# A gated linear recurrence feeding an exact-GELU feed-forward layer: decay totals by DMA, two units loaded by chunks, one PSUM pool, a new order

## The chip, the cores and the metric

The kernel runs on one core of one Trainium2 chip. The metric is the time of one execution on the device in microseconds (us), inputs and output in the chip's memory. Five engines work side by side, each on its own list of instructions in order: TensorE (PE, matmuls), VectorE (DVE), ScalarE (ACT), GpSimd (POOL) and SyncE (SP). In this kernel SP does nothing but issue DMAs, and an SP instruction that waits holds back every DMA listed behind it.

## The reference

```python
def _attn_ref(q, k, v, f_logit):              # (4, 8, 768, 48) each
    B, H, S, D = q.shape
    f = 1.0 / (1.0 + np.exp(-f_logit))
    state = np.zeros((B, H, D, D), dtype=np.float32)
    y = np.zeros_like(q)
    for t in range(S):
        state = f[:, :, t, :, None] * state + np.einsum('bhd,bhe->bhde', k[:, :, t], v[:, :, t])
        y[:, :, t] = np.einsum('bhd,bhde->bhe', q[:, :, t], state)
    return y

def _moe_ref(x, w_in, w_out):                 # (3072, 384), (384, 2048), (2048, 384)
    h = x @ w_in
    g = 0.5 * h * (1.0 + erf(h / np.sqrt(2.0)))
    return g @ w_out

x = attn_out.transpose(0, 2, 1, 3).reshape(B * S, H * D)   # then _moe_ref(x, ...)
```

## The kernel before

**Tiling.** The 4 x 768 tokens make 24 chunks of 128 tokens, six to a batch, numbered 0 to 23; two chunks make a unit, 0 to 11, so each batch has three units and the state starts anew with units 0, 3, 6 and 9. Unit u is also group u of the feed-forward part.

**One unit's attention.** `decays(u)` takes exp and ln of the logits (E, L; lines 559 and 561), and PE sums the logarithms along the chunk with a triangular matrix (C; line 585, or 590 and 591). ACT makes two factors from the sums, `rg` = exp(-G) (RG, line 607) and `gt` = exp(G) (GT, line 613). k times rg and q times gt go to `sc` (KP and QP, line 640, on DVE, a few on POOL), v becomes bf16 `vb` (VC, line 647, mostly POOL). `turn` brings `sc` into `kq` with channels on the partitions: for units 0 to 3 by PE transposes (line 876) and a copy from PSUM, for units 4 to 11 by a transposing DMA from SP (KD, line 864). From `kq` PE makes the scores (A), DVE masks them (AM, line 901), and PE multiplies them with `vb` (Y). The state goes on: PE forms k'v (S), DVE adds the old state (R, line 925), POOL multiplies by the decay total of the chunk, `gl` (T, line 927), and POOL copies the result as bf16 `sb` (SB, line 932), which the next chunk's Y takes up (line 969 on PE). The first chunk of a batch has no old state, and DVE multiplies by `gl` at once (R, line 921). `yb` is the bf16 copy of Y (YB, line 945); it is turned into `xT` by PE and a copy (XT and X, lines 961 and 964) or by a transposing DMA (XD, line 949, units 5 to 11).

**Decay totals.** For a chunk that stands with its tokens on the partitions, four matmuls with one column each (line 587) put the totals, channel by channel, into the PSUM bank of C, and ACT takes their exp into `gl` (line 629). Units in `PAIRS` (0 to 4) are loaded differently: partition p holds tokens 2p and 2p+1 of the unit, which makes one transfer of 384 KB per input with runs of 384 bytes (line 513). Their sums, scores and products have forms of their own: 590 and 591, totals at 579 with ACT at 634, scores at 1058 or 1061, S at 1093 (1085 in batch 0), Y at 1113, the old state at 975 or 978. The other units take two transfers of 192 KB per input, with runs of 192 bytes (line 521).

**Feed-forward.** Group g's 256 tokens go through two rounds: F1 (line 1165) in 8 tiles of 6 matmuls with 256 columns, each followed by one GELU on ACT (GE, line 1175), and F2 (line 1186) in 4 parts of 4 matmuls for each chunk, then a copy (O, line 1191) and a store (line 1200). After a unit in `PAIRS` the GELU also puts the tokens back in order. ACT's exp/ln and GELU lie in two tables, and each change of table is an instruction (line 1248).

**What sets the order.** Every piece of work is recorded with `P.add` (engine, planned duration, reads, writes, buffers), and `Plan.run` places the pieces one after another in the order of the numbers in `ORDER`. The instructions of each engine then stand in that order, and the plan's times also choose which buffer a piece gets. The planned durations and landing times (`d`, `lat`, `lag`) act on nothing else. PSUM has eight banks, `BANKS = (4, 0, 4)`: four for the feed-forward part and some early tiles (`s_fh`), four for all else (`s_m`, also used as `s_ap`). Loads are issued on SP in the order of `LOADS`; the weights come by POOL's DMAs (win at 525, wout at 528), and the first load of unit 3 waits until the third piece of wout, o3, has landed. At the start, while PE waits for data, line 1241 fills it with matmuls on a `junk` tile.

Of the kernel before, what the change touches and what calls it, by code (L numbers as in the profile page):

```python
# [11 lines left out]
ALU = mybir.AluOpType  # L12
# [9 lines left out]
TURN = 0.1  # L22
# [5 lines left out]
BANKS = (4, 0, 4)  # L28
# [47 lines left out]
class Plan:  # L76
# [30 lines left out]
    def run(self):  # L107
# [16 lines left out]
        while ready:  # L124
# [63 lines left out]
PAIRS = [0, 1, 2, 3, 4]  # L188
# [30 lines left out]
SBT = []  # L219
AHEAD = 4.4  # L220
UNITS = 12
WARM = 30.0
# [39 lines left out]
def kernel(  # L262
# [56 lines left out]
    s_gt, s_rg = slots(3, [C, HD], F32, "gt"), slots(3, [C, HD], F32, "rg")  # L319
# [13 lines left out]
    s_fh, s_m = Slots(nf, banks[:nf]), Slots(8 - nf - na, banks[nf + na:])  # L333
# [34 lines left out]
    P.add("POOL", 1.9, pair_sums, wr=["trip", "negp"], prio=-100)  # L368
    P.add("POOL", 2.6, pair_mask, wr=["maskp"], prio=-85)
# [9 lines left out]
    for i in range(6):  # L379
        P.add("DVE", 0.07, lambda i=i: nc.vector.memset(s_gl.tiles[i], 1.0), wr=[f"glz{i}"], prio=-60)  # L380
    z_gl = [f"glz{i}" for i in range(6)]
    z_lf = [f"lfz{i}" for i in range(3)]
# [24 lines left out]
    def load(eng, issue, wr, bufs, dur, name):  # L407
# [22 lines left out]
        if prev is not None and eng != "act" and order[-1][0] != eng:  # L430
            prev.lat = 2.2
# [18 lines left out]
        if 7 <= i and o.lat < 1.8:  # L450
            o.lat = 2.0 if name == "i0" else 1.8 if i < 30 else 1.7
# [23 lines left out]
    for what in LOADS:  # L475
# [12 lines left out]
        elif what[0] in "ucfkqv":  # L488
# [13 lines left out]
            elif x["pair"]:  # L502
                assert what[0] != "c"
                for nm, a in names:
                    if what[0] not in ("u", nm[0]):
                        continue
                    if nm == "fl" and m in SPLIT:
# [7 lines left out]
                        [(nm, 2 * m), (nm, 2 * m + 1)], [x[nm]], 1.5, f"{nm}{m}")  # L515
            else:
                for j in js:
                    for nm, a in names:
                        if what[0] not in ("u", "c", nm[0]):
                            continue  # L520
                        load("sp", lambda x=x, nm=nm, a=a, m=m, j=j: nc.sync.dma_start(
                            out=half(m, x[nm], j), in_=src(a, 2 * m + j)),
                            [(nm, 2 * m + j)], [x[nm]], 1.05, f"{nm}{m}.{j}")
        elif what[0] == "i" and m < len(WIN):
            load("pool", lambda m=m: nc.gpsimd.dma_start(out=win[m], in_=win_src[:, :, wcol[m]:wcol[m] + WIN[m]]),
                 [f"win{m}"], [], {512: 2.4, 1024: 4.1}[WIN[m]] + (0.3 if order[-1][0] == "sp" else 0.0), what)
        elif what[0] == "o":
            load("pool", lambda m=m: nc.gpsimd.dma_start(out=wout[m], in_=wo_src[m]), [f"wout{m}"], [], 2.15, what)


    def decays(u):
# [32 lines left out]
        g1d, gld = pair and u in G1D, u in GLD  # L564
# [717 lines left out]
```

## Time and profile before

| | |
|---|---|
| time of three runs | 179.1, 179.34, 180.19 us (median 179.34) |
| profiled execution | span 178.1 us; of its time no more is recorded than this span |
| PE, ACT, DVE, POOL busy | 168.7, 130.0, 93.7, 55.2 us |
| PE instructions | 1996 matmuls, 1996 weight loads |
| F1 and F2 (lines 1165, 1186) | 576 and 368 matmuls, 69.0 and 67.0 us busy |
| GELU | 96, 57.2 us busy |
| table changes on ACT | 17, and one load at the start, 1.283 us each |
| DMA | 32.61 MB in 106997 packets, 102112 of them under 512 bytes |

The page gives the busy time of each engine, the chain of work that ended last, and groups of instructions by line of the code. Matmuls overlap, so the busy time of a group of matmuls is more than what the group adds to PE's list; the pieces of the chain, which run from start to start, tell that. "idle before, releaser" says what an engine waited for.

### The profile page before, as it was taken

The numbers are of one execution on the slowest core, as the hardware profiler recorded it, in microseconds if no ns is written. First come the engines' busy times: TensorE is split into PE (matmuls) and PEld (weight loads), VectorE is DVE, ScalarE is ACT, GpSimd is POOL, SyncE is SP. The second block draws the span as 40 slices with busy tenths as digits, with TensorE's granted clock in tenths as the row PEclk, the third lists the DMA queues.
The fourth block names the chain that finished last, engine by engine and source line by source line (L and its number), as shares of the span: only waits on it lengthen the run. The fifth ranks groups of instructions, "written<-read, shape, count | busy, mean of one in ns | idle before, by whom it ended". The sixth has DMA issues, their size and how long they took to land.

```text
span 178.1 us, 4916 instructions
## 1 busy us (share of the span) xinstructions
PE 168.7 (95%) x1996; PEld 131.2 (74%) x1996; DVE 93.7 (53%) x188; ACT 130.0 (73%) x221; POOL 55.2 (31%) x119
## 2 busy tenths in 40 slices
PE   7787889999997999999999999999999999999993
PEld 2345679866787787886688689866797976887972
DVE  5188750067988556338677681246582276560110
ACT  2954399967797999989477597786684789951630
POOL 7267595041126801501052334002222504410000
PEclk9999999999999999999999999999999999999999
DMA  5999999999979898988999999999899975405412
GB/s 140 261 261 214 277 179 195 213 221 256 235 154 227 187 212 188 202 178 169 233 174 248 188 174 204 188 220 156 191 238 179 232 165 81 85 4 112 138 60 88
DMA packets 106997, 32.61 MB, mean 183 GB/s; under 512 B 102112, under 2 KB 106080, under 8 KB 106976
## 3 DMA queue, kind: packets, MB, share of 16 engines
q1 hardware_dynamic: 105056, 29.07, 79.0%
q0 software_dynamic: 1776, 3.15, 10.0%
q8 instruction: 15, 0.25, 0.6%
q10 hardware_dynamic: 144, 0.10, 0.2%
q14 instruction: 6, 0.05, 0.1%
HBM read 25.17 MB, written 4.72 MB: 168 GB/s over the span
## 4 chain that ended last, share of the span: by engine, by line
PE 72%; DMA 14%; SPq 6%; POOL 3%; issue 1%; DVE 1%; ACT 0%; DVEq 0%; POOLq 0%
PE ps L1165 30%; PE ps L1186 29%; DMA vt<-in_v_dram 6%; SPq L513 4%; DMA kt<-in_k_dram 4%; DMA kq<-sc 3%; PE ps L995 2%; PE ps L1031 2%; PE ps L1211 1%; DMA out_dram<-osb 1%; PE ps L585 1%; PE ps L969 1%; SPq L949 1%; SPq L1200 1%; POOL vb L647 1%
## 5 line engine op out<-in xcount | busy, mean ns | idle before, releaser
L1175 ACT ACTIVATE gT<-ps 128x512 bf16<-128x512 f32 x96 | 57.2, 665 | 18.4 <-PE ps L1165 17.6
L1165 PE MATMUL ps<-xT,win 128*128 128x256 bf16 x576 | 69.0, 273 | 0.8 <-DMA win<-in_moe_w_in_dram 0.7
L1186 PE MATMUL ps<-wout,gT 128*128 128x384 bf16 x368 | 67.0, 326 | 0.0
L1165 PEld LDWEIGHTS <-win 128*128 128x128 bf16 x576 | 61.7, 114 | 3.7 <-DMA win<-in_moe_w_in_dram 0.9
L1186 PEld LDWEIGHTS <-gT 128*128 128x128 bf16 x368 | 34.1, 98 | 18.7
L901 DVE TENSOR_TENSOR am<-ps,mask 128x512 bf16<-128x512 f32 x28 | 17.5, 683 | 18.5 <-PE ps L995 18.5
L1248 ACT ACT_TABLE_LOAD x17 | 21.8, 1283 | 0.3
L640 DVE TENSOR_TENSOR sc<-kt,rg 128x384 bf16<-128x384 f32 x19 | 11.5, 606 | 15.8 <-ACT rg L607 11.1
L1191 DVE COPY osb<-ps 128x384 f32<-128x384 f32 x20 | 10.7, 552 | 16.8 <-PE ps L1186 15.7
L927 POOL TENSOR_TENSOR tn<-rr,gl 128x384 f32<-128x384 f32 x12 | 10.7, 889 | 25.1 <-DVE rr L925 19.1
L647 POOL CAST vb<-vt 128x384 bf16<-128x384 f32 x18 | 9.5, 539 | 26.8 <-DMA vt<-in_v_dram 26.6
L901 DVE TENSOR_TENSOR am<-ps,maskp 128x512 bf16<-128x512 f32 x20 | 12.7, 683 | 5.3 <-PE ps L1061 3.8
L945 DVE CAST yb<-ps 128x384 bf16<-128x384 f32 x21 | 11.4, 555 | 7.6 <-PE ps L1031 5.6
L640 DVE TENSOR_TENSOR sc<-qt,gt 128x384 bf16<-128x384 f32 x20 | 13.3, 684 | 3.4 <-ACT gt L613 2.7
L558 ACT ACTIVATE fl<-fl 128x768 f32<-128x768 f32 x12 | 10.1, 842 | 5.0 <-DMA fl<-in_f_logit_dram 5.0
L932 POOL CAST sb<-tn 48x192 bf16<-48x192 f32 x30 | 10.7, 362 | 8.3 <-DVE tn L921 7.1
L613 ACT ACTIVATE gt<-ps 128x384 f32<-128x384 f32 x21 | 10.3, 495 | 3.8 <-PE ps L587 2.9
L607 ACT ACTIVATE rg<-ps 128x384 f32<-128x384 f32 x21 | 10.1, 494 | 3.5 <-PE ps L587 2.9
L640 POOL TENSOR_TENSOR sc<-kt,rg 128x384 bf16<-128x384 f32 x5 | 5.3, 1065 | 22.5 <-ACT rg L607 14.3
L561 ACT ACTIVATE lf<-fl 128x768 bf16<-128x768 f32 x12 | 10.2, 849 | 0.3
L925 DVE TENSOR_TENSOR rr<-ps,tn 128x384 f32<-128x384 f32 x12 | 6.7, 555 | 5.9 <-PE ps L1018 4.8
L1241 PE MATMUL ps<-junk 128*128 128x512 bf16 (+3 forms) x26 | 8.3, 448 | 1.3 <-POOL junk L1233 1.3
(85 smaller groups left out, 145.1 us busy)
## 6 DMA issues: line engine op xcount, KB each, us to landing
out_dram<-osb SPq DMA_DIRECT2D x19, 192.0 KB, 2.8
kt<-in_k_dram SPq DMA_DIRECT2D x14, 192.0 KB, 4.5
fl<-in_f_logit_dram SPq DMA_DIRECT2D x14, 192.0 KB, 3.9
vt<-in_v_dram SPq DMA_DIRECT2D x14, 192.0 KB, 3.9
qt<-in_q_dram SPq DMA_DIRECT2D x14, 192.0 KB, 3.7
fl<-in_f_logit_dram SPq DMA_DIRECT2D x5, 384.0 KB, 4.9
kt<-in_k_dram SPq DMA_DIRECT2D x5, 384.0 KB, 6.2
qt<-in_q_dram SPq DMA_DIRECT2D x5, 384.0 KB, 6.3
```

The lines of the kernel that those rows point to most:

```text
L613: P.add("ACT", 0.40, lambda g=gps[j], gtv=gtv: nc.scalar.activation(gtv(), g.t()[:, 0:HD].rearrange("q (p h d) -> q p h d", h=2, d=D), AF. ...
L640: P.add("POOL" if pl else "DVE", 0.80 if pl else 0.475, lambda a=a, y=y, j=j, w=w, pl=pl, b=(gtv if w else rg): (nc.gpsimd if pl else nc.v ...
L647: P.add("ACT" if hv else "POOL", 0.40 if hv else 0.47, lambda y=y, j=j, hv=hv: (nc.scalar.copy if hv else nc.gpsimd.tensor_copy)(y["vb"].t ...
L901: P.add("POOL" if pl else "DVE", 1.15 if pl else 0.61, lambda hh=hh, pl=pl: (nc.gpsimd if pl else nc.vector).tensor_tensor(ams[hh].t(), ap ...
L927: P.add("POOL", 0.83, lambda: nc.gpsimd.tensor_tensor(tn.t(), rr.t(), glb(), ALU.mult), rd=[("rr", n), ("gl", n)], wr=[("tn", n)], bufs=[r ...
L932: P.add("POOL", 0.36, lambda hh=hh: nc.gpsimd.tensor_copy(sb.t()[64 * hh:64 * hh + D, :, D * hh:D * hh + D], tn.t()[64 * hh:64 * hh + D, : ...
L945: P.add("ACT" if help_ else "DVE", 0.40 if help_ else 0.475, lambda: copier(help_)(yb.t()[:, i, :], yp.t()[:, 0:HD]), rd=[("yp", n)], wr=[ ...
L1165: nc.tensor.matmul(hps.t()[:, i * tok:(i + 1) * tok].rearrange("a (s t) -> a s t", s=s), col(fo)[:, kk, :], xT.t()[:, :, kk, :], start=(kk ...
L1175: nc.scalar.activation(to, fr, AF.Gelu)
L1186: nc.tensor.matmul(op.t()[:, 0:d_model], gT.t()[:, fo, s_ * C:(s_ + 1) * C], wout[fo // 4][:, fo % 4, :], start=(fo == 0), stop=(fo == FO ...
L1191: P.add("DVE" if od else "ACT", 0.475 if od else 0.40, lambda op=op, osb=osb, od=od: copier(not od)(osb.t(), op.t()[:, 0:d_model]), rd=[(" ...
L1248: nc.scalar.preload_act_table_set({"exp": "natural_log_exp_and_others", "gelu": "gelu_and_others"}[o.table])
```

## The change

It has five parts and a new table of order. Unit numbers are those of the code, counted from 0.

1. **Decay totals** (`GLD`): for units 5 to 11 the four one-column matmuls and ACT's exp of the totals go. `gt` of the chunk's last token already is the total, on one partition; a DMA on SP of 2 KB (128 pieces of 16 bytes) spreads that row over `gl`'s partitions (GD). It needs another layout of `gt`: head half, channel padded to 64, head pair, so that ACT writes and DVE or POOL read every fourth fp32 word. The last chunk of a batch needs no total, which leaves 11 such DMAs.
2. **Units 3 and 4** leave `PAIRS`: they are loaded by 16 transfers of 192 KB in place of 8 of 384 KB, and take the forms of the later units. They keep the totals by matmul.
3. **`XDMA`** gains unit 4: one more transposing DMA from `yb`, six PE transposes and two copies fewer.
4. **`AJ`**: the scores of both chunks of a unit are one block of PE's list for units 2 to 11 (before: 2, 4, 5, 7, 10, 11).
5. **`BANKS`**: all eight PSUM banks are one pool.
6. **The planner's durations** were set anew and the table `ORDER` is another one. The load of the exp table that opens the program stands in another place of the plan, so ACT loads it once more, after the logits of unit 2.

```diff
-BANKS = (4, 0, 4)
+BANKS = (8, 0, 0)
...
-                d += TABLE
+                t = max(t, free["ACT"] + TABLE)
...
-PAIRS = [0, 1, 2, 3, 4]
+PAIRS = [0, 1, 2]
...
-XDMA = [5, 6, 7, 8, 9, 10, 11]
+XDMA = [4, 5, 6, 7, 8, 9, 10, 11]
-AJ = [2, 4, 5, 7, 10, 11]
+AJ = [2, 3, 4, 5, 6, 7, 8, 9, 10, 11]
-GLD = []
+GLD = [5, 6, 7, 8, 9, 10, 11]
...
-5 6 2 8 18 10 26 30 0 9 7 13 12 16 24 19 27 31 17 121 15 11 14 32 122 129 33 192 34 130 123 125 133 22 35 38 193 131
+17 34 21 13 11 25 27 5 23 35 132 26 15 9 7 133 2 203 28 36 10 37 22 14 134 38 18 39 204 6 8 41 40 140 141 12 205 24
...
-    s_gt, s_rg = slots(3, [C, HD], F32, "gt"), slots(3, [C, HD], F32, "rg")
+    s_gt, s_rg = slots(3, [C, 512 if GLD else HD], F32, "gt"), slots(3, [C, HD], F32, "rg")
...
+    for i in range(3 if GLD else 0):
+        P.add("DVE", 0.1, lambda i=i: nc.vector.memset(s_gt.tiles[i][:, HD:512], 1.0), wr=[f"gtz{i}"], prio=-59)
...
-        g1d, gld = pair and u in G1D, u in GLD
+        g1d, gld = pair and u in G1D, not pair and u in GLD
...
-                    return gt.t().rearrange("q (h d p) -> q p h d", h=2, d=D)
-                return gt.t().rearrange("q (p h d) -> q p h d", h=2, d=D)
+                    return gt.t().rearrange("q (h d p) -> q p h d", h=2, d=64)[:, :, :, 0:D]
+                return gt.t()[:, 0:HD].rearrange("q (p h d) -> q p h d", h=2, d=D)
...
+                if n != last:
+                    P.add("DMA", 0.5, lambda gt=gt, j=j: nc.sync.dma_start(
+                        out=gl.t()[:, j, :], in_=gt.t()[C - 1:C, :].rearrange("o (h p) -> o h p", p=P2)),
+                        rd=[("gt", n)] + z_gl + z_gt, wr=[("gl", n)], bufs=[gt, gl], prio=-6.5, lag=1.7, lat=2.0, name=f"GD{n}")
...
-                P.add("DMA", 1.5, lambda sc=sc, j=j: nc.sync.dma_start_transpose(
+                P.add("DMA", 1.25, lambda sc=sc, j=j: nc.sync.dma_start_transpose(
```

Whole program: PE goes from 1996 to 1860 matmuls; SP gains 20 DMAs (8 loads, 11 small ones, one transposing); ACT has nine instructions fewer.

Three places show how the order moves. The first is ACT after the logits of unit 2 (E and L, lines 558 and 561 before, 569 and 572 now). Before:

```order
L558 ACTIVATE fl_91<-fl_91 128x768
L561 ACTIVATE lf_94<-fl_91 128x16x48
L1248 ACT_TABLE_LOAD
L1175 ACTIVATE gT_167<-ps_174 128x4x2x64
L964 COPY xT_164<-ps_175 128x384
L1175 ACTIVATE gT_167<-ps_172 128x4x2x64
```

Now, up to the first GELU:

```order
L569 ACTIVATE fl_91<-fl_91 128x768
L572 ACTIVATE lf_94<-fl_91 128x16x48
L348 ACT_TABLE_LOAD
L618 ACTIVATE rg_116<-ps_171 128x384
L624 ACTIVATE gt_114<-ps_171 128x384
L618 ACTIVATE rg_117<-g_125 128x384
L624 ACTIVATE gt_115<-g_125 128x384
L974 COPY xT_164<-ps_176 128x384
L639 ACTIVATE gl_121<-ps_171 128x4
L1258 ACT_TABLE_LOAD
L1185 ACTIVATE gT_167<-ps_177 128x4x2x64
```

Unit 2's factors (rg, gt, gl), which stood behind sixteen GELUs, now stand ahead of the first one, together with the copy of xT, and a second load of the same exp table stands ahead of them. On DVE, in the same place, unit 2's subtraction (line 599) now stands ahead of the second yb copy of unit 1, and a QP of unit 2 ahead of the copy of xT.

The second place is POOL at units 3 and 4: VC of chunks 6 and 7 (vb from unit 3's vt_85), KP of chunk 8 (from unit 4's kt_77), then the state of chunk 6. Before:

```order
L647 CAST vb_110<-vt_85 128x384
L640 TENSOR_TENSOR sc_95<-kt_77,rg_117 128x8x48
L647 CAST vb_111<-vt_85 128x384
L932 CAST sb_153<-tn_146 48x4x48 x2
L927 TENSOR_TENSOR tn_147<-rr_139,gl_122 128x384
```

Now:

```order
L652 CAST vb_110<-vt_85 128x384
L652 CAST vb_112<-vt_85 128x384
L645 TENSOR_TENSOR sc_95<-kt_77,rg_116 128x8x48
L942 CAST sb_153<-tn_146 48x4x48 x2
L937 TENSOR_TENSOR tn_141<-rr_140,gl_122 128x384
```

The second cast of unit 3 no longer stands behind KP of chunk 8, which needs unit 4's k.

The third place is SP, around the loads of units 6 and 7 (qt_84 is unit 6's, qt_83 and fl_90 are unit 7's) and the turns of unit 5 (KD, into kq_129). Before:

```order
L521 DMA qt_83<-in_q_dram 128x8x48 x2
L521 DMA qt_84<-in_q_dram 128x8x48
L864 DMA_TRANSPOSE kq_129<-sc_97 128x8x128
L864 DMA_TRANSPOSE kq_129<-sc_98 128x8x128
L521 DMA qt_84<-in_q_dram 128x8x48
L521 DMA fl_90<-in_f_logit_dram 128x8x48 x2
```

Now:

```order
L529 DMA qt_83<-in_q_dram 128x8x48 x2
L529 DMA qt_84<-in_q_dram 128x8x48
L629 DMA gl_124<-gt_113 128x1x4
L529 DMA qt_84<-in_q_dram 128x8x48
L959 DMA_TRANSPOSE xT_164<-yb_156 128x6x128
L529 DMA fl_90<-in_f_logit_dram 128x8x48
L1210 DMA out_dram<-osb_158 128x384
L874 DMA_TRANSPOSE kq_129<-sc_97 128x8x128
L1210 DMA out_dram<-osb_161 128x384
L874 DMA_TRANSPOSE kq_129<-sc_98 128x8x128
```

The first of the eleven small DMAs (GD of chunk 10, which waits for ACT's GT) and the added transposing DMA of unit 4 now stand ahead of a load of unit 6 and of unit 5's turns.

More of the change, by code (lines that the diff above doesn't have):

```diff
@@ L219 @@
 SBT = []
+VCE = {}
+FM = []
+TE = {}
+SBE = {}
+SBD = {"POOL": 0.38, "DVE": 0.22, "ACT": 0.27}
 AHEAD = 4.4
 UNITS = 12
+LANDS = {"i0": 2.2, "kt4": 3.4}
 WARM = 30.0
@@ L332 @@
     nf, na, _ = BANKS
-    s_fh, s_m = Slots(nf, banks[:nf]), Slots(8 - nf - na, banks[nf + na:])
+    s_fh = Slots(nf, banks[:nf])
+    s_m = Slots(8 - nf - na, banks[nf + na:]) if nf + na < 8 else s_fh
     s_ap = Slots(na, banks[nf:nf + na]) if na else s_m
@@ L522, with copy_on @@
                             out=half(m, x[nm], j), in_=src(a, 2 * m + j)),
-                            [(nm, 2 * m + j)], [x[nm]], 1.05, f"{nm}{m}.{j}")
+                            [(nm, 2 * m + j)], [x[nm]], 0.82, f"{nm}{m}.{j}")
         elif what[0] == "i" and m < len(WIN):
             load("pool", lambda m=m: nc.gpsimd.dma_start(out=win[m], in_=win_src[:, :, wcol[m]:wcol[m] + WIN[m]]),
-                 [f"win{m}"], [], {512: 2.4, 1024: 4.1}[WIN[m]] + (0.3 if order[-1][0] == "sp" else 0.0), what)
+                 [f"win{m}"], [], {512: 1.95, 1024: 4.1}[WIN[m]] + (0.35 if order[-1][0] == "sp" else 0.0), what)
         elif what[0] == "o":
-            load("pool", lambda m=m: nc.gpsimd.dma_start(out=wout[m], in_=wo_src[m]), [f"wout{m}"], [], 2.15, what)
+            load("pool", lambda m=m: nc.gpsimd.dma_start(out=wout[m], in_=wo_src[m]), [f"wout{m}"], [], 1.87, what)
+    def copy_on(eng):
+        return {"ACT": nc.scalar.copy, "POOL": nc.gpsimd.tensor_copy, "DVE": nc.vector.tensor_copy}[eng]
     def decays(u):
@@ L610, in gtv @@
                 if gld:
[L611 to L613 removed]
+                    return gt.t().rearrange("q (h d p) -> q p h d", h=2, d=64)[:, :, :, 0:D]
+                return gt.t()[:, 0:HD].rearrange("q (p h d) -> q p h d", h=2, d=D)
+            P.add("ACT", 0.375, lambda g=gps[j], gtv=gtv: nc.scalar.activation(
                 gtv(), g.t()[:, 0:HD].rearrange("q (p h d) -> q p h d", h=2, d=D), AF.Exp),
[L615 removed]
+                  rd=[("g", n)] + (z_gt if gld else []), wr=[("gt", n)], bufs=[gps[j], gt], table="exp", prio=pr + 1, name=f"GT{n}")
             if gld:
[L617 to L626 removed]
+                if n != last:
+                    P.add("DMA", 0.5, lambda gt=gt, j=j: nc.sync.dma_start(
+                        out=gl.t()[:, j, :], in_=gt.t()[C - 1:C, :].rearrange("o (h p) -> o h p", p=P2)),
+                        rd=[("gt", n)] + z_gl + z_gt, wr=[("gl", n)], bufs=[gt, gl], prio=-6.5, lag=1.7, lat=2.0, name=f"GD{n}")
             elif not pair:
@@ L645, in decays @@
                     port=True, name=f"{nm.upper()}{n}")
-            hv = u in HVC
-            P.add("ACT" if hv else "POOL", 0.40 if hv else 0.47, lambda y=y, j=j, hv=hv: (nc.scalar.copy if hv else nc.gpsimd.tensor_copy)(
+            hv = VCE.get(n, "ACT" if u in HVC else "POOL")
+            P.add(hv, {"ACT": 0.40, "POOL": 0.47, "DVE": 0.3}[hv], lambda y=y, j=j, hv=hv: copy_on(hv)(
                 y["vb"].t().rearrange("p (h d) -> p h d", h=H), half(u, x["vt"], j)),
@@ L900, in mask_scores @@
                 continue
-            P.add("POOL" if pl else "DVE", 1.15 if pl else 0.61, lambda hh=hh, pl=pl: (nc.gpsimd if pl else nc.vector).tensor_tensor(
+            P.add("POOL" if pl else "DVE", 1.15 if pl else 0.605, lambda hh=hh, pl=pl: (nc.gpsimd if pl else nc.vector).tensor_tensor(
                 ams[hh].t(), aps[hh].t().rearrange("p (h t) -> p h t", t=C),
@@ L1158, in ffn_group @@
         for u in range(FO // pk):
-            hps = s_fh.new()
+            hps = (s_m if (g, u) in FM else s_fh).new()
             def f1(u=u, hps=hps):
@@ L1175, in gelu @@
                 nc.scalar.activation(to, fr, AF.Gelu)
-            P.add("ACT", 0.60 if perm(ns[0]) and ns[0] // 2 not in RST else 0.50, gelu, rd=[("h", g, u)], wr=[("gT", g, u)], bufs=[hps, gT], table="gelu", prio=pr - 1000,
+            P.add("ACT", 0.585 if perm(ns[0]) and ns[0] // 2 not in RST else 0.49, gelu, rd=[("h", g, u)], wr=[("gT", g, u)], bufs=[hps, gT], table="gelu", prio=pr - 1000,
                   name=f"GE{'q' * (s == 4)}{g}.{u}")
@@ L1200, in store @@
                     nc.sync.dma_start(out=out[rc[n] * C + r:rc[n] * C + r + w, :], in_=osb.t()[r:r + w, :])
-            P.add("DMA", 1.25 if perm(n) and n // 2 in RST else 0.6, store, rd=[("os", n)], bufs=[osb], prio=-5, lag=4.0, name=f"st{n}")
+            P.add("DMA", 1.25 if perm(n) and n // 2 in RST else 0.55, store, rd=[("os", n)], bufs=[osb], prio=-5, lag=4.0, name=f"st{n}")
         for i, eng in enumerate(("ACT", "DVE") if first[g] + s == NCH else ()):
```

66 lines of the change are left out of this document (29 added, 37 removed), and 60 rows, old and new, of the table ORDER.

## The prediction

> **What bounds the kernel now.** I read the busy time by stretches first, then PE's waits, then the chain that ended last.
>
> ```profile
> PE 168.7 (95%) x1996; PEld 131.2 (74%) x1996; DVE 93.7 (53%) x188; ACT 130.0 (73%) x221; POOL 55.2 (31%) x119
> 25.00:53.00 28.00, 28.00 (x351) 22.52 (x349) 14.70 (x28) 24.31 (x44) 7.70 (x18) 1.00 1.01 208
> 53.00:55.00 2.00, 1.06 (x22) 0.81 (x21) 1.65 (x4) 2.00 (x4) 1.30 (x2) 1.00 0.88 218
> 55.00:159.00 104.00, 103.92 (x1175) 83.06 (x1174) 59.58 (x107) 83.33 (x141) 30.45 (x57) 1.00 0.92 181
> 159.00:178.00 19.00, 16.00 (x136) 12.77 (x132) 2.40 (x5) 5.89 (x12) 0.00 (x0) 1.00 0.35 94
> PE ps L1093 <- POOL vb L647: 0.9, 1, 0.9
> 45.31 7.07 DMA kt<-in_k_dram
> 54.35 0.52 PE ps L1093 x16
> ```
>
> In the rows of stretches the columns are stretch, length, PE, PEld, DVE, ACT, POOL, granted clock, DMA share and GB/s. From 25 to 159 us PE is full at a granted clock of 1.00, but for one hole: unit 4's k lands at 52.38, POOL multiplies it, then casts unit 3's v, and only then S of unit 3 (line 1093) starts, 0.94 late. So behind 25 us only three things count: work taken off PE, the moment at which PE becomes full, and waits. DVE and POOL have room. ACT, at 83 of 104 us, and the DMA engines, at a share of 0.92, have little.
>
> **Work taken off PE.** Pieces of the chain run from start to start, so they price a group in PE's list, overlap taken out.
>
> ```profile
> 66.29 0.16 PE ps L585
> 66.45 0.08 PE ps L587 x4
> 43.94 0.19 PE ps L579 x8
> 70.39 0.17 PE ps L961 x3
> 56.96 0.45 PE ps L1093 x16
> 72.03 0.17 PE ps L1018 x4
> 67.20 0.51 PE ps L1113 x32
> 81.17 0.20 PE ps L1031 x8
> 67.71 0.46 PE ps L978 x16
> 81.00 0.17 PE ps L969 x4
> 63.63 0.57 PE ps L1061 x32
> 78.11 0.55 PE ps L995 x16
> 78.66 0.78 PE ps L1165 x6
> 95.62 0.67 PE ps L1165 x6
> ```
>
> - Totals: 28 matmuls of line 587 go (44 to 16), at 0.02: -0.56. Line 579 goes from 40 to 24: -0.38.
> - Units 3 and 4 in the late form. S: 32 of 1093 go (-0.90), 16 of 1018 come (+0.68). Y: 64 of 1113 go (-1.02), 32 of 1031 come (+0.80). Old state: 16 of 978 (-0.46) and 4 of 975 (as 969, -0.17) go, 12 of 969 come (+0.51). Scores: 64 of 1058 and 1061 go (-1.14), 32 of 995 come (+1.10). Sums: four matmuls of 384 columns for four, 0. Together -0.60.
> - XD of unit 4 takes six transposes of line 961: -0.34.
> - The F1 tile behind a block of scores takes 0.78 where another takes 0.67: PE pays 0.11 on leaving such a block. The blocks of this kind (scores, and S and Y in the pair form) go from 15 to 11 behind 25 us: -0.45. Joined scores by themselves give little, since most already stood side by side.
>
> Sum -2.3; ends -1.9 (no turn saved) and -2.8 (0.11 on entering too). Beside that, six F1 matmuls (0.109 each) and four transposes of unit 2 (0.056 each) move ahead of 25 us, where PE has holes: -0.9, ends -0.5 and -1.0.
>
> **The start.** Unit 2's factors now stand ahead of the first GELU.
>
> ```profile
> 23.95 0.56 DVE L945 CAST yb<-ps 128x384 bf16<-128x384 f32 x1 [0.21 <-PE ps L975]
> 22.71 1.28 ACT L1248 ACT_TABLE_LOAD   x1
> 24.00 0.76 ACT L1175 ACTIVATE gT<-ps 128x512 bf16<-128x512 f32 x1
> 24.92 3.44 PE L1165 MATMUL ps<-xT,win 128*128 128x256 bf16 x30
> 32.43 2.53 ACT L1175 ACTIVATE gT<-ps 128x512 bf16<-128x512 f32 x4 [0.28 <-PE ps L1165]
> 36.27 0.52 ACT L607 ACTIVATE rg<-g 128x384 f32<-128x384 f32 x1
> 36.70 0.47 ACT L607 ACTIVATE rg<-ps 128x384 f32<-128x384 f32 x1
> 37.07 0.48 ACT L613 ACTIVATE gt<-ps 128x384 f32<-128x384 f32 x1
> ```
>
> ACT's second load of the exp table falls where the GELU table was loaded, 22.71 to 23.99, and mostly into a wait for C of unit 2. Then come RG, GT, RG, GT at 0.4 apart (36.27 to 37.07), X and GL, until 26.0, the GELU table until 27.3, and the first GELU there, 3.3 later than the 24.00 of before. On DVE the subtraction, a piece of the same size (0.56), goes between the two yb copies: the second ends at about 25.0 in place of 24.51, the transposes of unit 1 follow, and then a QP of some 0.7 ahead of the copy of xT. F1 of group 1 starts at about 26.1, where the stream of F1 started at 24.92 to 25.08: +1.0. Ends 0 (the two DVE pieces fit into waits) and +1.8 (every piece a little later, and the first GELU with them).
>
> The late GELUs are covered by the banks: with eight in one pool F1 can run seven tiles ahead, and GELUs follow each other at 0.59 ((2.53 - 0.76)/3), F1 tiles at 0.655. From 27.3 they keep up but for a copy of kq among them: +0.2, ends 0 and +0.8. If the cover goes, PE stands as long as ACT is late. Behind that, the one pool is priced at 0: PE's rows show no wait for a bank that it could take away, and a bank held longer than planned would cost PE one output copy, 0.5.
>
> **Units 3 and 4.** POOL's new order takes the 0.94 away. What is late next is unit 4's last k itself: S of chunk 9 now stands early in PE's list, behind unit 3's scores, at about 54.7 by the prices above.
>
> ```profile
> 38.00:44.00 6.00, 6.00 (x97) 4.03 (x96) 4.67 (x8) 4.21 (x6) 1.94 (x6) 1.00 1.18 274
> 63.00:68.00 5.00, 5.00 (x111) 3.89 (x109) 2.48 (x4) 4.98 (x7) 0.51 (x1) 1.00 1.11 220
> kq<-sc SPq DMA_TRANSPOSE x16, 3.8
> out_dram<-osb ACTq DMA_DIRECT2D x1, 96.0 KB, 1.7
> 125.76 0.57 SPq L1200 DMA_DIRECT2D out_dram<-osb  x1
> 132.97 1.26 SPq L949 DMA_TRANSPOSE xT<-yb  x1
> ```
>
> The first two rows are of stretches; their last column gives 274 GB/s while transfers of 384 KB run and 220 while 192 KB ones do. 3.15 MB take 11.5 us at the one and 14.3 at the other: 2.8 more, though the smaller transfers land with less queued behind them. I take k at 53.5 (52 to 55) and KP on DVE 0.6 behind it: +0.3, ends 0 and +1.5. Behind a stalled S in PE's list stand F1 and F2 parts, so nothing fills the hole.
>
> **The small DMAs.** Removed from ACT: seven GLs. Added to SP: eleven issues, each waiting for a GT, with loads, KD and XD queued behind. No row shows such a DMA. By the rows nearest, the total lands 1.7 (one store) to 3.8 (a transposing DMA) after issue, at worst the 7.07 of k above. GD of chunk 10 follows C by some 3 us and T needs it only behind S of chunk 10, ten us of PE's list later; R of chunk 18 on DVE is the nearest use, some 4 us behind C, and may hold DVE for 1 to 2 us, which has 44 of 104 us free. What SP pays for an issue lies between the 0.57 of a store and the 1.26 of an XD, the smaller being the nearer in size. I take 0 on the path, ends 0 and +1. The added XD displaces copies and is covered by F2 of older groups: 0, ends -0.2 and +0.5.
>
> **Sum.** -2.3 - 0.9 + 1.0 + 0.2 - 0.94 + 0.3 + 0.2 for small waits of the new order = -2.4 (rounded). Against the execution's span: 178.1 to 175.7. The median of the runs is 179.34, 1.24 above that span, since a time takes in what lies around it; I take the same 1.24 and forecast 176.9. All good ends together give -4.9, all bad ones +2.5.
>
> **Rivals.**
> 1. *The saving is eaten by new waits.* The start costs its 1.8 and 0.8, unit 4's k its 1.5: -2.3 - 0.9 + 1.8 + 0.8 - 0.94 + 1.5 + 0.2 = +0.2, which is 179.5; half of the excess gives 178.3. For it: the order packs ACT's GELUs later and unit 4's transfers are slower. Against: eight banks, and room on DVE.
> 2. *Slower: the DMA engines become the bound.* Mechanism: eleven issues at 0.57 (row 125.76), one XD at 1.26 and 2.8 of slower loads make 10.3 us, all in one queue that no load of units 5 to 11 can leave. Its share between 55 and 159 is 0.92, so 8.3 of those 104 us are free. It decides once the added work is more than that: then the stretch lasts as long as its transfers, 2.0 us longer than now, and PE's shorter list brings nothing there: 179.34 + 2.0 = 181.3. Against: the loads run ahead of their use, PE is full in that stretch, and the share falls to 0.35 at the end, so that part of the work can move there.
> 3. *gt's wide layout.* A nearest row is the GELU that writes with a step:
>
> ```profile
> L1175 ACT ACTIVATE gT<-ps 128x512 bf16<-128x512 f32 x16 | 10.1, 764 | 0.3 <-PE ps L1165 0.3
> L1175 ACT ACTIVATE gT<-ps 128x512 bf16<-128x512 f32 x8 | 4.8, 597 | 1.6 <-PE ps L1165 1.4
> L640 DVE TENSOR_TENSOR sc<-qt,gt 128x384 bf16<-128x384 f32 x20 | 13.3, 684 | 3.4 <-ACT gt L613 2.7
> L629 ACT ACTIVATE gl<-ps 128x4 f32<-128x4 f32 x11 | 2.1, 190 | 2.0 <-DVE am L901 2.0
> ```
>
> In the first two, of GELUs, the first row (24 to 35 us) reorders tokens, the second (150 to 160 us) does not: 28% more. The same on 14 GTs (0.48, row 37.07) is 1.9 us of ACT and on 14 QPs (0.684) 2.7 of DVE and POOL; if ACT's part lies on the path, 178.8. Against: ACT loses 7 GLs of 0.19 and 16 reordering GELUs. The Trainium skill, "SBUF — State Buffer", section "Door 1: The DMA port swizzle (why `[64,N]` ≈ `[32,N]`)", says that SBUF has lines of 16 bytes and that every access that goes to a new line pays; a step of four fp32 words is just where that begins, so by that page each GT and QP here pays, and this rival is the page's. The rows above agree only in that a step costs; no run so far has this layout.
>
> **How the numbers follow.** Forecast 0.60, rival 1 0.25, rival 2 0.08, rival 3 0.07. One per cent, about what a measurement here tells from none, is 1.8 us: faster is below 177.55. Of the forecast's 0.60, 0.54 lies there and 0.06 above; of rival 1 0.04 faster, 0.20 the same, 0.01 slower; of rival 2 0.01 the same and 0.07 slower; of rival 3 0.02 and 0.05. Faster 0.60, same 0.32, slower 0.08. The range leaves out rival 2 and the outermost ends: 174.8 (the good ends of PE's work, of the start with its banks and of unit 4's k) to 179.6 (rival 1 in full).
>
> **What would show it.** Right: F1's stream from about 26 us, the first GELU near 27, no PE wait for vb of unit 3, PE full from 26 to 157, lines of the totals down to 16 and 24 matmuls. The forecast is wrong if PE shows waits of over 2 us together behind 26 us: on kt or S of chunk 9 near 55 (rival 1), on kq or xT behind late DMAs after 60 (rival 2), or if GT and QP in their wide form take over 0.6 and 0.85 (rival 3).

## The result, and the profile after

The changed kernel takes 192.38 us (median of four runs, 191.0 to 193.9) against 179.22 beside it: a ratio of 1.070, with a 95% interval of 1.063 to 1.077. It is 13 us slower, where 176.9 was forecast and the range ended at 179.6. Times in this document are medians of all runs of a kernel, ratios go by its undisturbed runs alone, and the profiled execution (span 191.9) is a disturbed one whose granted clock fell to 0.86 from 150 to 160 us, so its stretches and its chain are read ahead of 150.

Engines first (busy time, share, instructions), from the page of the changed kernel:

```profile
PE 171.3 (89%) x1860; PEld 130.4 (68%) x1860; DVE 97.1 (51%) x188; ACT 130.7 (68%) x212; POOL 58.6 (31%) x119
```

Then the stretches, with the columns of the prediction. First the changed kernel, then the kernel before over the stretch in which loads are still on their way:

```profile
25.00:53.00 28.00, 27.07 (x316) 21.70 (x317) 12.90 (x26) 25.32 (x46) 7.80 (x16) 1.00 0.98 185
55.00:145.00 90.00, 80.82 (x863) 62.89 (x862) 54.52 (x94) 67.17 (x105) 27.34 (x49) 1.00 1.01 192
```

```profile
55.00:145.00 90.00, 89.92 (x1018) 72.14 (x1017) 50.63 (x93) 71.62 (x124) 25.81 (x49) 1.00 1.01 200
```

Between 55 and 145 us PE stood for 0.1 us before and for 9.2 now. ACT, DVE and POOL have room in both. The DMA share is 1.01 in both, and the engines that move data now move 192 GB/s where they moved 200. That 1.01 is their limit is not shown: a_tot_st below reaches 1.11 and 205 GB/s over the same stretch. From 25 to 53 us they move 185 where the prediction's row has 208. Together that is some 1.4 MB less, near 7 us at 200 GB/s (an estimate from these rows). SP's list has no room either: by the lengths of its instructions in the traces, SP spends 81.7 of the 90 us from 55 to 145 on issuing DMAs before, and 83.3 now. The prediction asked for room on every engine but this one.

What PE waited for, from its waits in the changed kernel (us in total, times, longest):

```profile
PE ps L596 <- ACT lf L572: 5.3, 3, 2.5
PE ps L979 <- ACT osb L1201: 1.8, 1, 1.8
...
PE ps L971 <- DVE yb L955: 1.1, 2, 0.7
PE ps L886 <- POOL sc L645: 1.0, 2, 0.6
...
PE ps L1005 <- DMA kq<-sc: 0.9, 2, 0.7
```

The first two come from ACT, which is not at its limit. The chain of waits shows what ACT stood for (start, us, what):

```profile
63.87 1.09 SPq L529
65.01 0.70 SPq L529
65.75 3.37 DMA out_dram<-osb
69.25 0.33 issue
69.58 0.86 ACT fl L569
...
88.89 4.99 DMA fl<-in_f_logit_dram
93.96 0.85 ACT fl L569
94.83 0.85 ACT lf L572
95.73 0.32 PE ps L596
...
141.33 5.78 DMA fl<-in_f_logit_dram
147.14 0.85 ACT fl L569
148.01 0.85 ACT lf L572
148.91 0.32 PE ps L596
```

At 63.9 a store stands behind loads on SP and is issued at 65.75; ACT's copy of an output needs the buffer that it frees, and with the copy wait the logits of unit 6. At 88.89 and 141.33 the logits themselves are in flight for 5 us or more, E and L follow, and PE gets its C only then. ACT's waits for logits, in the kernel before and in the changed one:

```profile
ACT fl L558 <- DMA fl<-in_f_logit_dram: 5.0, 2, 2.6
```

```profile
ACT fl L569 <- DMA fl<-in_f_logit_dram: 15.6, 5, 4.4
```

Both of the first lie ahead of 21 us, at the start. In the kernel before the last logits were issued at 138.69 and used at 144.62, with ACT busy up to then; now they are issued 2.6 later and ACT stands for them. So these late units start when their loads land. Of the operations that the change touches, GT from 55 to 175 us, QP on DVE over the whole span, and the small transfers (KB, us to landing):

```profile
L624 ACT ACTIVATE gt<-ps 128x384 f32<-128x384 f32 x14 | 11.7, 885 | 1.7 <-PE ps L596 1.6
```

```profile
L645 DVE TENSOR_TENSOR sc<-qt,gt 128x384 bf16<-128x384 f32 x20 | 17.4, 885 | 10.0 <-ACT gt L624 7.9
```

```profile
gl<-gt SPq DMA_DIRECT2D x11, 2.0 KB, 2.6
```

GT in its wide layout takes 0.885, where it took 0.496, and QP's mean went from 0.684 to 0.885. A small transfer lands 2.6 us after its issue.

### The profile page after: what moved, and what is told of

Same layout as the page of the kernel before. It is cut to its first block, busy times and chain, and to the rows that moved or that the text cites. A ratio compares the mean times of both kernels' runs of the same rounds, so it can differ in the third digit from the quotient of the medians.

```text
span 191.9 us, 4674 instructions
## 1 busy us (share of the span) xinstructions
PE 171.3 (89%) x1860; PEld 130.4 (68%) x1860; DVE 97.1 (51%) x188; ACT 130.7 (68%) x212; POOL 58.6 (31%) x119
## 4 chain that ended last, share of the span: by engine, by line
PE 43%; DMA 18%; SPq 14%; ACT 13%; DVE 6%; issue 5%; ACTq 0%; DVEq 0%
PE ps L1175 19%; PE ps L1196 17%; DMA fl<-in_f_logit_dram 11%; SPq L529 6%; SPq L521 5%; ACT gT L1185 3%; DMA out_dram<-osb 3%; SPq L874 3%; ACT L1258 2%; ACT gt L624 2%; DVE sc L645 2%; DVE am L911 2%; ACT fl L569 2%; DMA xT<-yb 2%; DMA kt<-in_k_dram 2%
## 5 line engine op out<-in xcount | busy, mean ns | idle before, releaser
L1196 PE MATMUL ps<-wout,gT 128*128 128x384 bf16 x368 | 69.4, 331 | 0.5 <-ACT gT L1185 0.5
L1185 ACT ACTIVATE gT<-ps 128x512 bf16<-128x512 f32 x96 | 53.1, 680 | 16.6 <-PE ps L1175 16.2
L911 DVE TENSOR_TENSOR am<-ps,mask 128x512 bf16<-128x512 f32 x36 | 22.7, 682 | 10.9 <-PE ps L1005 10.1
L645 DVE TENSOR_TENSOR sc<-qt,gt 128x384 bf16<-128x384 f32 x20 | 17.4, 885 | 10.0 <-ACT gt L624 7.9
L624 ACT ACTIVATE gt<-ps 128x384 f32<-128x384 f32 x23 | 16.0, 735 | 2.3 <-PE ps L596 1.6
L942 POOL CAST sb<-tn 48x192 bf16<-48x192 f32 x30 | 13.0, 440 | 9.0 <-DVE tn L931 5.4
L618 ACT ACTIVATE rg<-ps 128x384 f32<-128x384 f32 x23 | 11.2, 511 | 2.7 <-PE ps L596 2.1
L596 PE MATMUL ps<-lf,trin 128*128 128x384 bf16 x18 | 5.6, 336 | 5.3 <-ACT lf L572 5.3
L1251 PE MATMUL ps<-junk 128*128 128x512 bf16 (+2 forms) x28 | 9.1, 452 | 1.3 <-POOL junk L1243 1.3
L886 PE MATMUL ps<-ident,sc 128*128 128x128 bf16 x64 | 5.9, 220 | 2.6 <-POOL sc L645 1.0
```

What stands on the lines that cost most here:

```text
L618: P.add("ACT", 0.375, lambda g=gps[j], rg=rg: nc.scalar.activation(rg.t(), g.t()[:, 0:HD], AF.Exp, scale=-1.0), rd=[("g", n)], wr=[("rg", ...
L624: P.add("ACT", 0.375, lambda g=gps[j], gtv=gtv: nc.scalar.activation(gtv(), g.t()[:, 0:HD].rearrange("q (p h d) -> q p h d", h=2, d=D), AF ...
L645: P.add("POOL" if pl else "DVE", 0.92 if pl else 0.475, lambda a=a, y=y, j=j, w=w, pl=pl, b=(gtv if w else rg): (nc.gpsimd if pl else nc.v ...
L911: P.add("POOL" if pl else "DVE", 1.15 if pl else 0.605, lambda hh=hh, pl=pl: (nc.gpsimd if pl else nc.vector).tensor_tensor(ams[hh].t(), a ...
L942: P.add("POOL", 0.38, lambda hh=hh: nc.gpsimd.tensor_copy(sb.t()[64 * hh:64 * hh + D, :, D * hh:D * hh + D], tn.t()[64 * hh:64 * hh + D, : ...
L1185: nc.scalar.activation(to, fr, AF.Gelu)
```

## The experiments

Three theories stand against each other. *Layout*: the slower GT and QP lose the time. *Transfers*: what the change adds to SP's list does, either by SP's own time (the issue theory) or by the time of the DMA engines (the engine theory). *Order*: the new list of numbers does, which counts on events that come later than planned.

Every time below stands beside runs of the kernel before on the same chip; ratios carry 95% intervals. Runs whose name begins with b start from the kernel before and keep its order; those with a start from the changed kernel.

### One part at a time, in the old order

**b_wide**, the layout of `gt` alone:

```diff
+                if not pair:
+                    return gt.t().rearrange("q (h d p) -> q p h d", h=2, d=64)[:, :, :, 0:D]
```

> The kernel before, with gt of units 5 to 11 written and read in the changed kernel's layout (steps of 16 bytes) and nothing else. Layout theory: GT takes about 0.88 as in the changed kernel, 0.39 more on each of 14, QP about 0.2 more; if most of the loss comes from this, 182 to 190 us. Transfers theory and order theory: ACT had 11.7 us of waits behind 55 us and DVE more, so the wider writes alone give 179 to 181.

Measured: 179.82, ratio 1.004 (1.000 to 1.007). GT takes as long as in the changed kernel and it costs 0.6 us: in the old order ACT has the room, busy for 75.3 us of the 90 from 55 to 145. Layout falls as the main cause.

**b_split**, the loads of units 3 and 4 in short runs:

```diff
+                        w = D if m > 2 else 2 * D
+                        for o in range(0, 2 * D, w):
+                            i = nc.sync.dma_start(out=x[nm].t().rearrange("p (h x) -> p h x", h=H)[:, :, o:o + w],
+                                                  in_=srcp(a, m)[:, :, o:o + w])
```

> The kernel before, with the eight loads of units 3 and 4 each issued as two transfers of 192-byte runs, the number of packets that loading by chunks has. Transfers theory (the DMA engines are the bound): 2.8 us of slower loads and eight issues more come out as 182 to 185 us. Layout theory and order theory: 179 to 180.5.

Measured: 183.05, ratio 1.019 (1.011 to 1.027), 3.4 us. The edit adds eight issues as well as shorter runs, so it doesn't part the two. PE now waits 1.4 us for `kq` of unit 4, and 1.5 for `vb` of unit 3, where it waited 0.9.

**b_gd**, the small transfers alone:

```diff
+                    if w and not pair and n != last:
+                        nc.sync.dma_start(out=dump[:, n, :], in_=gt.t()[C - 1:C, :].rearrange("o (h p) -> o h p", p=P2))
```

> The kernel before, with the eleven 2 KB transfers of the changed kernel added behind the QPs, from gt in its old layout into a tile that nobody reads (the computation is unchanged). Transfers theory: eleven issues of 0.6 on SP that wait for GT, and their packets, cost 2 to 6 us: 181 to 185. Layout theory and order theory: 179 to 180.5.

Measured: 186.22, ratio 1.040 (1.034 to 1.047): 7.2 us for 22 KB that nobody reads, more than any theory had asked.

**b_banks**, `BANKS = (8, 0, 0)` alone:

> The kernel before in its old order, with one pool of eight banks for four and four. Banks never held PE up in the trace of before: 178.5 to 180.5. If a bank is held longer somewhere: 181 to 184.

Measured: 178.99, ratio 0.999 (0.995 to 1.002). The single pool is free.

### What a small transfer costs, and where

**b_gdpool** issues the same eleven from POOL (`nc.gpsimd.dma_start`):

> The kernel before with the same eleven 2 KB transfers into an unread tile, now issued by POOL and not by SP. Issue theory (SP's one list of issues is full, each issue on it and each wait in it delays every load behind): 179 to 180.5, where SP's version took 186.2. Engine theory (the transfers themselves take DMA time): 184 to 187, as from SP.

Measured: 179.22, ratio 0.997 (0.994 to 1.000). From there the transfers cost nothing, as the issue theory had it. **b_gdfree** leaves them on SP, but from a row that is ready (`in_=crow[C - 1:C, :]`):

> As b_gd (186.2), but the eleven small transfers from SP read a constant row, so that SP never waits for GT ahead of them; the computation is unchanged. If the 0.54 of each issue is the price (11 at 0.54 are 5.9): 183 to 186.5. If SP's waits for GT are (4.3 and 1.2 in the profile of b_gd): 179 to 181.5.

Measured: 184.62, ratio 1.028 (1.022 to 1.034). So 5.0 of the 7.2 us stay when SP waits for nothing, and some 2 seem to be SP's waits for GT (the two intervals just touch). Eleven issues at 0.54 are 5.9 us, so the size is the one that the issue theory gives.

The two runs differ in more than the queue. Packets, MB and share of the 16 engines, for SP's queue (kernel before, then b_gdfree) and for POOL's (kernel before, then b_gdpool):

```profile
q1 hardware_dynamic: 105056, 29.07, 79.0%
q1 hardware_dynamic: 106640, 29.10, 81.1%
```

```profile
q0 software_dynamic: 1776, 3.15, 10.0%
q0 software_dynamic: 2128, 3.17, 10.5%
```

From SP a transfer is 144 packets, by the trace 128 of 16 bytes and 16 of 4 bytes; from POOL it is 32, 16 of 128 bytes and 16 of 4. So b_gdpool changes the issuer and the pieces at once. The 16-byte packets took 7.8 ns each in b_gdfree, 0.7 us in all when spread over 16 engines, so their own time isn't the 5 us. The stretches from 55 to 145 us of b_gdfree and of b_gdpool:

```profile
55.00:145.00 90.00, 86.35 (x970) 68.53 (x971) 47.83 (x88) 67.69 (x118) 23.90 (x45) 1.00 1.03 186
```

```profile
55.00:145.00 90.00, 90.00 (x1035) 72.04 (x1033) 50.55 (x93) 72.68 (x125) 30.37 (x58) 1.00 1.00 198
```

With the small transfers in SP's queue 186 GB/s are moved at a share of 1.03; with them in POOL's queue, 198 at 1.00. Fourteen GB/s less than the 200 of before, over 90 us, are 1.26 MB, or 6.3 us at the old rate. In b_gd, where SP also waits for GT, the same stretch has 185 GB/s at a share of 0.95: the rate falls there while the engines are less busy.

**b_stpool** and **a_gdpool** take other issues off SP: the stores of the kernel before, the small transfers of the changed one.

```diff
-                    nc.sync.dma_start(out=out[rc[n] * C + r:rc[n] * C + r + w, :], in_=osb.t()[r:r + w, :])
+                    nc.gpsimd.dma_start(out=out[rc[n] * C + r:rc[n] * C + r + w, :], in_=osb.t()[r:r + w, :])
```

> The kernel before, with the 27 stores of whole chunks issued by POOL and not by SP, nothing else changed. Issue theory: SP's list gets 11 us freer between 50 and 150 us, but PE is full there already, so 177.5 to 179.5. Engine theory: the same transfers, 178.5 to 180. If POOL's own issues cost more than SP's, 180 to 183.

> The changed kernel, with the eleven transfers of totals issued by POOL and not by SP. Issue theory: 6 us of issues and the waits for GT leave SP's list, 185 to 189 of 192.4, near the 189.3 of the version without them. Engine theory: 191 to 193.

Measured: b_stpool 180.56, 1.005 (1.002 to 1.008); a_gdpool 191.22, 1.055 (1.049 to 1.060). Without the stores on SP the kernel before gains nothing, and POOL waits 11.9 us for the outputs that it stores. In the changed kernel moving the small transfers is worth about 1.4% (2.7 us), by the ratio between what the two theories asked, and not the 7.2 us of b_gd: other things are late there too.

**b_totpool** and **b_totpool2** do the first part of the change for real in the old order: no total matmuls, `gl` filled by small transfers from POOL. In the second each issue stands later in POOL's list.

```diff
-                    P.add("ACT", 0.19, lambda g=gps[j], j=j: nc.scalar.activation(
-                        gl.t()[:, j, :], g.t()[:, HD:HD + P2], AF.Exp),
+                    P.add("POOL", 0.1, lambda gt=gt, j=j: nc.gpsimd.dma_start(
+                        out=gl.t()[:, j, :], in_=gt.t()[C - 1:C, :].rearrange("o (h p) -> o h p", p=P2)),
```

> The kernel before with one part of the change alone: the totals of units 5 to 11 turned by the small transfers, issued by POOL and not by SP, with the wide gt; 44 one-column matmuls and eleven ACT exponentials go. Issue theory: the transfers are free on POOL, PE's list is 0.9 shorter (44 at 0.02), so 177.8 to 179. If T or R waits for a transfer that lands late: 179.5 to 182.

> As b_totpool (185.1), totals of units 5 to 11 by small transfers from POOL and no total matmuls, but each issue stands 2 us later in POOL's list, so that POOL doesn't wait for GT with casts and T behind it, and gt has four buffers. If POOL's waits were the price: 178 to 180.5. If the landing behind it is too late for R and T: 182 to 186.

Measured: 185.06, ratio 1.024 (1.019 to 1.030), and 180.46, ratio 1.006 (1.003 to 1.009). The first lies above both of its ranges. POOL's waits, first in b_totpool, then in b_totpool2:

```profile
POOL gl L633 <- ACT gt L617: 46.4, 8, 9.8
```

```profile
POOL gl L633 <- ACT gt L617: 13.2, 3, 8.7
...
POOL tn L931 <- DMA gl<-gt: 2.7, 1, 2.7
```

A wait on POOL holds back the casts and T behind it. Once most of it is gone 0.6% is left, and a T that waits for its total. Turned by DMA, the totals gain nothing even then.

### The parts together, and the order

**b_parts** is the kernel before, in its order, with the edits of b_wide, b_split and b_gd at once; **b_parts_st** adds the stores from POOL.

> The kernel before in its old order, with three parts at once: the loads of units 3 and 4 in 192-byte runs, the eleven small transfers from SP into an unread tile, the wide gt. Parts theory (what is added to SP's list loses the time, whatever the order): 189 to 193, the sum of 3.4, 7.2 and 0.6 on 179.6 or more. Order theory (the new order loses most): 183 to 187, since the parts' delays share the same slack.

> As b_parts (190.5), with the 27 stores of whole chunks issued by POOL: 10 us of issues between 50 and 150 leave SP's list, where eight loads and eleven small transfers were added. Issue theory (SP's list is what the parts overfill): 180.5 to 184.5. Engine theory (the transfers themselves are too many): 188 to 191.

Measured: b_parts 190.51, ratio 1.062 (1.056 to 1.068). The three ratios by themselves add up to 6.3%: they share no slack, and a loss nearly as large as the changed kernel's is there without its order. It is not the same loss: in the changed kernel the small transfers are worth 1.4% (a_gdpool) and not 4.0. PE's waits in b_parts are those of the second rival:

```profile
PE ps L1179 <- DMA xT<-yb: 4.8, 4, 2.2
PE ps L1075 <- DMA kq<-sc: 1.6, 1, 1.6
```

b_parts_st: 191.09, ratio 1.055 (1.050 to 1.060), not told from b_parts, and by the ratio in the range of the engine theory. Ten us of SP's issues less do not bring the time back, as the issue theory had asked. But full engines are not what b_parts shows:

```profile
55.00:145.00 90.00, 82.75 (x949) 65.05 (x949) 51.65 (x89) 69.88 (x115) 24.93 (x45) 1.00 0.98 185
```

The share is 0.98, less than the 1.01 of before, and 185 GB/s are moved. Nor is the run a clean one for the issue theory, since the stores on POOL have a price of their own there: POOL waits 12.6 us for the outputs, with casts and T behind. So neither theory, as worded, is shown by these two runs.

**a_tot** is the changed kernel without small transfers and without the wide layout; **a_widetot** keeps the wide layout; **a_tot_st** is a_tot with the stores from POOL.

```diff
-                    for p in range(0 if gld or n == last else P2):
+                    for p in range(0 if n == last else P2):
...
-            if gld:
-                if n != last:
-                    P.add("DMA", 0.5, lambda gt=gt, j=j: nc.sync.dma_start(
...
-            elif not pair:
+            if not pair:
```

> The changed kernel with its order, its chunk loads and its banks, but the totals of late units taken again by one-column matmuls and an ACT exponential behind GT, and gt in its old layout: no small transfer, no wide write. Layout theory: 178 to 182 us, GT back at 0.50. Transfers theory: half-way, 184 to 188, since the chunk loads and the added XD stay. Order theory: 187 to 192, with ACT still waiting over 10 us for fl loads and for the store that frees osb.

> The changed kernel with the wide gt kept but totals by matmul and an ACT exponential, so that it differs from the run a_tot by the layout of gt alone. Layout theory as it stands after the first runs (the wide writes cost nothing where ACT waits, and something where an order counts on 0.375 for each GT): 189 to 193 against 189.3. If the layout is the rest of the loss in the new order: 191.5 to 193.5. If it is free there too: 188.8 to 190.

> The changed kernel with totals by matmul and the old layout of gt (as in the run a_tot), and the stores of whole chunks issued by POOL: no store stands behind a load in SP's list, and none ahead of one. Issue theory: ACT's wait of 7.4 for the store that frees osb goes, loads come up to 9 us of issues earlier, 178 to 183. Engine theory (share of the DMA engines near 1.0, slower loads): 187 to 190. Order theory (PE's and ACT's lists in themselves): 187 to 190 with fl loads landing in time.

Measured: 189.33, ratio 1.056 (1.051 to 1.061); 192.54, ratio 1.068 (1.061 to 1.075); 187.78, ratio 1.044 (1.038 to 1.050). Without either, 10 us remain; in this order the wide layout seems to cost some 2 us, at the edge of what these intervals tell. The small transfers add nothing on top of it: beside them stand the matmuls and exponentials that they save. With the stores from POOL (a_tot_st) 1.2% less is lost than in a_tot, the intervals apart: in this order fewer issues on SP do help, if far less than the 178 to 183 us of the issue theory. The stretch of a_tot_st:

```profile
55.00:145.00 90.00, 84.17 (x927) 66.06 (x926) 53.72 (x95) 68.62 (x120) 34.05 (x62) 1.00 1.11 205
```

More is moved here than in the kernel before, and still PE stands for 5.8 us: in this order the rate alone is not what PE lacks. In a_widetot ACT still waits for logits and for the store, and the same two lead in a_tot:

```profile
ACT fl L569 <- DMA fl<-in_f_logit_dram: 11.6, 7, 3.1
ACT osb L1196 <- DMA out_dram<-osb: 6.8, 1, 6.8
```

**a_replan** has the operations of a_tot in an order made anew by a search with the planner's own rules, but with longer transfers:

```diff
-                            [(nm, 2 * m + j)], [x[nm]], 0.82, f"{nm}{m}.{j}")
+                            [(nm, 2 * m + j)], [x[nm]], 1.05, f"{nm}{m}.{j}")
...
-                P.add("DMA", 1.25, lambda sc=sc, j=j: nc.sync.dma_start_transpose(
+                P.add("DMA", 1.5, lambda sc=sc, j=j: nc.sync.dma_start_transpose(
```

> The operations of the run a_tot (189.3) in an order that was made anew with longer transfers: 1.05 for a chunk load in place of 0.82, 1.5 and 1.4 for the transposing ones in place of 1.25 and 1.15. Order theory (the new list counted on loads that come earlier than they do): 183 to 187. Parts theory (the chunk loads and the XD of unit 4 fill SP's list under any order): 188 to 191.

Measured: 185.21, ratio 1.032 (1.027 to 1.037), 4.3 us less than a_tot by the ratios, in the range of the order theory. The waits of ACT for logits fall, and the store is gone from them:

```profile
ACT fl L569 <- DMA fl<-in_f_logit_dram: 6.7, 4, 2.6
```

0.82 us for a chunk load is 192 KB at 240 GB/s. At the 220 of the prediction's row from 63 to 68 us, where such loads run alone, it is 0.89, and at the 200 from 55 to 145, with transposing transfers and stores between them, 0.98. The changed kernel's order counted on loads faster than either. How much of the 4.3 us is due to the durations is not shown: no run has an order searched anew with the old ones.

**g_old** and **g_new** leave the table out, so that the planner's rule alone sets the order (`ORDER = []`, `GLD = []`), with the parts of the kernel before and with the new ones (pairs, banks, XD, joined scores; totals by matmul).

> The changed kernel's program with its list of numbers left out, so that the planner's own rule sets the order, and with the parts of the kernel before: five units in pairs, four banks and four, XD from unit 5, totals by matmul, gt in its old layout. No theory says where this lies; 182 to 192. It is the base for the next run.

> The same rule for the order, with the new parts but without the small transfers and the wide gt: three units in pairs, one pool of eight banks, XD from unit 4, joined scores. Order theory (the new list of numbers loses the time, its parts do not): not slower than the run with the old parts, 3 to 8 us faster. Parts theory (chunk loads, XD and the pool lose it under any order): 2 to 8 us slower than that run.

Measured: 197.5, ratio 1.096 (1.090 to 1.102), and 196.33, ratio 1.092 (1.086 to 1.098). Under this rule the new parts are neither 2 us slower nor 3 faster; the intervals overlap. In an order this loose the loads may well be hidden, so the runs say little on either theory.

## Why the prediction was wrong

1. **The room on the DMA engines, misread.** The prediction set the added transfers against "8.3 of those 104 us", from a share of 0.92 between 55 and 159. Taken to 145 only, where the last loads end, the share before is 1.01. By the prediction's own measure, in which a share of 1 is full, the free time lay behind 145, where there is nothing left to load. This is the step that failed first. SP's list, the other thing that each load needs, was not asked for room at all: it was issuing for 81.7 of 90 us. "The loads run ahead of their use" was true by a few us only (138.69 to 144.62 for the last logits, landing included).
2. **"I take 0 on the path, ends 0 and +1"** for the small DMAs. In the old order they cost 7.2 us from SP, in the changed kernel 2.7 (a_gdpool). The prediction looked for their price in their landing and in the room of the engine that uses the total; it lies in the transfers behind them in SP's queue.
3. **"I take k at 53.5 (52 to 55)"**: unit 4's last k landed at 55.0, the late end of the range, and S of chunk 9 waited 0.5 in the changed kernel. But the term made slower loads a matter of that one wait (+0.3, ends 0 and +1.5). Alone they cost 3.4 us, near the 2.8 that the prediction itself had worked out for the queue.
4. **The second rival** had the direction, and that added transfers in SP's one queue delay what stands behind them; with a chance of 0.08 and a price of 2.0 it was set far too low. Its added work was 10.3 us; b_parts, in the old order, measures 11.1 (6.2%). That the two lie so close is luck in part, since b_parts has no XD of unit 4 and the wide layout instead. The 8.3 that it subtracted was not there while loads were still to come. That the DMA engines are what is full, as it says, is not shown. Its sign, over 2 us of waits on `kq` and `xT`, came in b_parts; in the changed kernel PE waits 1.4 on these and 5.3 on the sums behind late logits, a wait that no sign had named.
5. **"0.2 for small waits of the new order"** was a term without a row behind it. The order was taken as a list of positions. That its planned durations were cut (chunk loads from 1.05 to 0.82) stood in the diff, against rows of 220 and 200 GB/s. Remaking the order with longer transfers gave 4.3 us back.
6. **The work taken off PE**, -2.3 and -0.9, can't be read: with 136 matmuls fewer PE is busy for 171.3 us and not for 168.7, and its list is broken by waits. g_old and g_new differ by 1.2 us in that direction, inside their intervals. It stays open.
7. **The start** was right: 26.1 for F1's stream and 27.3 for the first GELU were forecast. In the changed kernel's timeline (start, us, engine, line):

```profile
26.81 1.47 PE L1175 MATMUL ps<-xT,win 128*128 128x256 bf16 x12
```

```profile
28.14 2.55 ACT L1185 ACTIVATE gT<-ps 128x512 bf16<-128x512 f32 x4
```

   Both are 0.7 to 0.8 later than forecast, as far as the bad ends reach. The wait for `vb` of unit 3 is all but gone (0.2), and the banks cost nothing in b_banks, as priced.
8. **The third rival** was right about the operations and more than it priced: GT went up by 78% and not by 28%, beyond the bounds of 0.6 and 0.85 named as its sign. The rule of the Trainium skill, "SBUF — State Buffer", section "Door 1: The DMA port swizzle (why `[64,N]` ≈ `[32,N]`)", that each new 16-byte line is paid for, goes with that row. But the sign was no proof: the same slow GT costs 0.6 us in the old order and some 2 in the new one, so the rows of an operation tell what it takes, not what it is worth.

What stays open: why a 2 KB transfer in SP's queue takes about 0.5 us from the loads around it. Its issue by SP fits in size (0.54), and SP's list was full; against it stands that stores taken off SP gave nothing back in b_parts_st, and only 1.2% in a_tot_st. The issue of one load of logits lasts from 0.43 to 2.85 us in the kernel before (14 loads of 192 KB), so SP itself may be held up by what is queued; the traces don't tell. No run keeps SP as the issuer and changes the pieces, or takes other issues off SP in b_gdfree. Open too is what the chunk loads cost in the new order, which no run undoes, and with it the 3.2% left in a_replan: 1.9% is what they cost in the old order; the XD of unit 4 was not tried alone, and another order may be better. No version here beats the kernel before: b_banks and b_gdpool can't be told from it.

## What to carry to other kernels

Read the DMA share over the stretch in which loads are still to come, not up to the end of the work: 0.92 was 1.01 there. Add up the issues of the engine that issues the loads too: SP was issuing for 81.7 of 90 us, and each added transfer delayed the loads behind it, whoever waited for it. Put a small transfer in a queue that carries no loads, and not ahead of work that must be prompt. And where a diff changes the planned durations of an order, divide bytes by duration and hold it against the rate in the profile: 240 GB/s were planned, 220 were there with loads alone and 200 with other transfers between.

## What the runs showed of the hardware

Eleven transfers of 2 KB took 5 us from a full SP queue with no one waiting on them, and nothing measurable when POOL issued them. From SP each was 128 packets of 16 bytes and 16 of 4 (b_gdfree), from POOL 16 of 128 bytes and 16 of 4 (b_gdpool). The Trainium skill, "DMA: Bandwidth & Descriptors", section "Issuing engines are not separate DMA queues", says that issuing from several engines only saves the time of the issue, since all transfers run on the same DMA engines. b_gdfree and b_gdpool differ by some 5 us, and eleven issues of 0.54 are 5.9, which agrees; that the pieces differ too, and that fewer stores on SP saved nothing in the old order, keeps these runs from showing it. Loads of 192 KB ran alone at 220 GB/s in runs of 192 bytes (63 to 68 us of the kernel before), loads of 384 KB at 274 in runs of 384 bytes (38 to 44 us). ACT's write with a step of 16 bytes took 0.885 us for 128 x 384 fp32 where the contiguous write took 0.496.
